# GLA recurrence then squared-ReLU FFN on one Trainium2 core: dense rows for q and k, on-chip transposes for the last decays of blocks 0 to 3, and another order of the opening

## The chip, the cores and the metric

The kernel runs on one core of a Trainium2 chip. The core has a matrix engine (TensorE, called PE in the profile, with its weight loads shown apart as PEld), three engines for elementwise work (VectorE or DVE, ScalarE or ACT, GpSimd or POOL), and SyncE (SP), which here only issues DMAs. The metric is the device time of one execution in microseconds (us); lower is better. Each engine works off its own instructions in the order in which the program lists them and waits on semaphores for the others, so the order of the program text is the order of work on every engine.

## What is computed

```python
def _attn_ref(q, k, v, alpha):                 # each [4, 8, 768, 48], float32
    B, H, S, D = q.shape
    state = np.zeros((B, H, D, D), dtype=np.float32)
    for t in range(S):
        state = alpha[:, :, t, :, None] * state + np.einsum('bhd,bhe->bhde', k[:, :, t], v[:, :, t])
        y[:, :, t] = np.einsum('bhd,bhde->bhe', q[:, :, t], state)

def _moe_ref(x, w_in, w_out):                  # x = y as [3072, 384]; 384 -> 2048 -> 384
    h = np.maximum(x @ w_in, 0.0)
    return (h * h @ w_out).astype(np.float32)
```

The two weights arrive as float64; the queries, keys, values and alphas as float32.

## The kernel before

**Blocks.** The 768 steps of a sequence are cut into 6 chunks of 128 steps (C). A block n is one chunk of one of the 4 batches, so there are 24 blocks, and blocks 0 to 3 (GB = 4) are the first chunk of all batches. A block works with its 128 steps on the partitions and its 8 heads of 48 columns in the free dimension. Four blocks make a group of 512 tokens; the FFN runs group by group, and the attention of the next group is woven into the FFN of the current one.

**The steps of a block.** With b the running product of the alphas inside the chunk, these are, by the names that the hand-written list uses:
- `load`: DMAs from SP of alpha (a), q, k and v of the block, 192 KB each (L109).
- `ln` (L244): ACT takes the logarithm of alpha. `cs` (L265): TensorE sums the logarithms over time by one matmul with a triangular matrix of ones, into a PSUM bank of 512 columns, of which the sums fill 384. `eb` and `ei` (L276, L280): ACT takes exp of plus and minus the sums, which are b and 1/b (`inv`).
- `mq` and `mk` (L284): DVE multiplies q by b and k by 1/b in place.
- `bl` and `br` (L297, L303): the last row of b is the decay of the state over the whole chunk. It is needed with the 48 key dimensions on the partitions, a column for each head pair. `bl` writes the row (1536 bytes) from SBUF to a row in DRAM, and `br` reads it back with two DMAs into `last`, transposed by its addresses. All three are issued by SP.
- `kT`, `qT` (L309): four TensorE transposes each, of 128x128, so that two heads of 64 columns (48 used) make one transpose; `kc`, `qc` (L325) copy the result from PSUM to SBUF, on DVE for block 0 and on ACT otherwise.
- `sc` (L372) multiplies keys by queries, `am` (L380) is DVE's masked copy of these scores, `kv` (L395) sums keys by values, `us` (L406) adds the state before the chunk on DVE, and `st` (L420, L421) forms the new state on DVE: it adds the second half of the sums and multiplies by `last`.
- `ya`, `yb` (L352): y of two blocks on TensorE, in two parts with a hop through POOL (L456) between them. `ev` (L515) copies this y from PSUM into x, the FFN's input, by six copies on DVE and the others on ACT for the pairs beginning with blocks 0 and 2.

**Dense and wide rows.** The transposes take 128 columns, two heads of 64, so q and k are kept in tiles of 8 heads of 64 columns, whose columns 48 to 63 POOL sets to zero once at the start (L97 and its like). The loads of q and k write 48 of every 64 columns of such a tile; the loads of a and v write tiles of 384 columns without gaps. Blocks 2 and 3 borrow their tiles from pools that the FFN uses later.

**The FFN.** Its input weights come as 8 pieces of 128x768 in float64 (768 KB, `weights`). A piece is turned into float32 by three steps: `first` (L153, L157, two DVE operations on the high words), `middle` (L166, L169, two ACT operations) and `second` (L175, L179, L182, three DVE operations). The first layer of group 0 multiplies in float32 (`ffn_in`, L806): output row block j of 16 needs weight piece j/2 and the x of the whole group, three matmuls of 512 columns. For j = 0 and 1 each is split into a half for blocks 0 and 1 (`ha`) and a half for blocks 2 and 3 (`hb`), so that the first halves can run before the second y is there. Later groups use three-pass matmuls on parts of the operands (L623, L702), with the weights' parts kept in DRAM and streamed back. Relu and square of h are then done by ACT and DVE in one of several mixes (L638, L640, L652, L657, L661), named by the letters in `AT['tp']`, one letter for j modulo 4.

**The order.** The opening, up to the first full matmuls of the FFN, is the list `first` (lines 852 to 861): words such as `cs1` or `load3q`, called from left to right. For instance its last lines in the kernel before are

```python
        weights2 qT3 sc2 load4q qc3 kv2 second0 am2 br3 first1 sc3 weights3 us2
        load4a kv3 am3 us3 load4k middle1 ha1 second1 ya2 yb2 ev2 weights4 first2
        ha0 hb1 middle2 hb0 st2 st3 st1
```

`warm` and `zeros` (L221, L338) are matmuls on tiles of zeros whose result is never used; they fill TensorE's waits. After the list, `weave` walks through the FFN's units, each with a cost, and slips in the other work (attention of the next blocks, weight conversions) when the running cost passes a position. These positions are the numbers of the table `AT` in line 19.

## Time and profile before

The median of 3 runs is 519.17 us (518.97 to 519.44). The profile is of one execution of its own.

| quantity | us |
| --- | --- |
| time of the profiled execution | 519.41 |
| its span, first to last instruction | 517.6 |
| DMA q1, share of 16 engines over the span | 70.0% |

| stretch (us) | PE busy | DVE busy | ACT busy | POOL busy |
| --- | --- | --- | --- | --- |
| 0 to 5.6 | 4.33 | 1.83 | 1.80 | 4.74 |
| 5.6 to 14 | 6.44 | 4.36 | 4.47 | 0.60 |
| 14 to 36 | 19.58 | 18.62 | 12.37 | 0 |
| 140 to 254 | 113.66 | 93.28 | 77.89 | 0 |
| 254 to 514 | 259.98 | 161.93 | 131.24 | 0 |

Times inside an execution are counted from the start of the span. A line of a timeline gives the start, the duration of the run of instructions, the engine, the line of the kernel, the operation and its tiles, and in brackets how long the engine was idle just before and who ended that wait. A matmul's end is modelled, so a busy PE is not PE at its peak. The row PEclk of the page, the granted TensorE clock in tenths, is 9 (90% or more) throughout; the mean granted clock is 1.000. Loads are listed by tile with the time at which they landed; "lands" below is that time.

### The profile page before, as it was taken

Reading aid. Unit: us, or ns where it says so; the run is one execution under the profiler, and the core shown is the slowest. Engines: PE = TensorE matmul, PEld = TensorE weight load, DVE = VectorE, ACT = ScalarE, POOL = GpSimd, SP = SyncE. Lnnn points to the kernel's source line nnn. Section 1 sums busy time; section 2 is a strip of 40 time slices with the busy share of each in tenths; the row PEclk is TensorE's granted clock in tenths of the full one; section 3 lists DMA queues with packets and bytes.
Section 4 is the critical chain, followed back from the end, with each engine's and each line's share of the span. In section 5 each row is a group of like instructions: output and inputs, shape, how many; then the busy total and the mean of one; then the engine's idle time right before and its main releaser. Section 6 shows DMA issues by size and latency. Waiting matters only on the chain.

```text
span 517.6 us, 12956 instructions
## 1 busy us (share of the span) xinstructions
PE 508.0 (98%) x5292; PEld 420.5 (81%) x5292; DVE 370.0 (71%) x639; ACT 303.9 (59%) x638; POOL 5.3 (1%) x29
## 2 busy tenths in 40 slices
PE   7989999999999999999999999999999999999997
PEld 4754455668878689988899988899988899988996
DVE  4698989996898898875888176778165578164861
ACT  4658786766788766176954175955075754154620
POOL 4000000000000000000000000000000000000000
PEclk9999999999999999999999999999999999999999
DMA  9999777262699688898965888865774544898201
GB/s 158 206 267 219 209 232 227 61 185 110 220 262 208 186 214 217 294 334 200 272 158 176 253 241 210 231 161 152 247 241 124 183 126 151 271 349 290 66 1 62
DMA packets 141283, 103.15 MB, mean 199 GB/s; under 512 B 111508, under 2 KB 114600, under 8 KB 141224
## 3 DMA queue, kind: packets, MB, share of 16 engines
q1 hardware_dynamic: 141224, 102.32, 70.0%
q8 instruction: 42, 0.69, 0.6%
q14 instruction: 17, 0.14, 0.1%
HBM read 84.97 MB, written 17.33 MB: 198 GB/s over the span
## 4 chain that ended last, share of the span: by engine, by line
PE 91%; DMA 4%; ACT 2%; SPq 1%; DVE 1%; issue 0%; DVEq 0%
PE o L702 41%; PE h L623 31%; PE h L806 7%; PE y L352 4%; PE sckv L372 2%; PE T L482 2%; PE sckv L395 2%; DMA row<-b 1%; DMA a_lent<-in_alpha_dram 1%; DMA a_in<-in_alpha_dram 1%; DMA k_in<-in_k_dram 1%; PE cs L265 1%; DVE x L515 1%; PE cs L268 0%; PE cs L269 0%; SPq L109 0%
## 5 line engine op out<-in xcount | busy, mean ns | idle before, releaser
L638 ACT ACTIVATE hid<-h 128x512 f32<-128x512 f32 x40 | 24.0, 602 | 81.6 <-PE h L623 81.5
L623 PE MATMUL h<-xa,wb 128*128 128x512 f32 x240 | 68.3, 393 | 0.0
L623 PE MATMUL h<-xl,wl 128*128 128x512 f32 x240 | 67.6, 390 | 0.0
L623 PE MATMUL h<-xd,wd 128*128 128x512 f32 x240 | 67.2, 395 | 0.0
L515 ACT COPY x<-y 32x256 f32<-32x256 f32 (+2 forms) x132 | 47.5, 365 | 26.8 <-PE y L352 21.6
L702 PE MATMUL o<-wb,ha 128*128 128x384 f32 x168 | 57.4, 342 | 0.0
L702 PE MATMUL o<-wd,hd 128*128 128x384 f32 x320 | 56.4, 334 | 0.0
L702 PE MATMUL o<-wl,hl 128*128 128x384 f32 x168 | 56.2, 335 | 0.0
L702 PEld LDWEIGHTS o<-wd,hd 128*128 128x128 f32 x320 | 55.6, 188 | 0.0
L623 PEld LDWEIGHTS h<-xl,wl 128*128 128x128 f32 x240 | 45.0, 188 | 9.8
L623 PEld LDWEIGHTS h<-xd,wd 128*128 128x128 f32 x240 | 44.3, 188 | 9.5
L623 PEld LDWEIGHTS h<-xa,wb 128*128 128x128 f32 x240 | 44.6, 188 | 8.7
L702 PE MATMUL o<-wb,hx 128*128 128x384 f32 x152 | 51.3, 338 | 0.0
L702 PE MATMUL o<-wl,hx 128*128 128x384 f32 x152 | 50.8, 334 | 0.0
L806 PE MATMUL h<-x,w_in 128*128 128x512 f32 (+1 forms) x108 | 43.6, 552 | 1.2 <-ACT x L515 1.2
L702 PE MATMUL o<-w_out,hid 128*128 128x384 f32 x128 | 43.4, 491 | 0.0
L547 DVE TENSOR_TENSOR osb<-o,osb 128x384 f32<-128x384 f32 x24 | 13.2, 555 | 39.9 <-PE o L702 31.0
L547 DVE TENSOR_TENSOR hid<-h,hid 128x512 f32<-128x512 f32 x40 | 27.4, 687 | 18.9 <-PE h L623 18.8
L806 PEld LDWEIGHTS h<-x,w_in 128*128 128x128 f32 x108 | 19.9, 190 | 21.1 <-issue 17.2
L702 PEld LDWEIGHTS o<-w_out,hid 128*128 128x128 f32 x128 | 23.8, 190 | 15.3
L597 ACT ACTIVATE ha<-hid 128x512 fp32r<-128x512 f32 x42 | 26.6, 641 | 15.6 <-DVE hx L598 8.8
L598 DVE SCALAR_TENSOR_TENSOR hl<-ha,hid 128x512 fp32r<-128x512 f32 x42 | 28.7, 684 | 6.4 <-ACT ha L597 6.4
(113 smaller groups left out, 886.7 us busy)
## 6 DMA issues: line engine op xcount, KB each, us to landing
wd<-do SPq DMA_DIRECT2D x38, 384.0 KB, 4.3
wl<-lo SPq DMA_DIRECT2D x34, 384.0 KB, 3.9
wl<-li SPq DMA_DIRECT2D x32, 384.0 KB, 4.9
wd<-di SPq DMA_DIRECT2D x32, 384.0 KB, 5.0
raw<-in_moe_w_in_dram SPq DMA_DIRECT2D x8, 768.0 KB, 6.3
raw<-in_moe_w_out_dram SPq DMA_DIRECT2D x8, 768.0 KB, 6.8
v_in<-in_v_dram SPq DMA_DIRECT2D x24, 192.0 KB, 5.4
out_dram<-osb SPq DMA_DIRECT2D x24, 192.0 KB, 4.4
```

The lines of the kernel that those rows point to most:

```text
L352: ins = nc.tensor.matmul(out=ys[e][64 * half : 64 * half + D + G * e, m % 2, p // 2, t], lhsT=lhsT, rhs=rhs, start=(half, e) not in seen, ...
L372: nc.tensor.matmul(out=ps[e][HALF[h], 0, p, :], lhsT=ks[rows, p, HALF[h]], rhs=qs[rows, p, HALF[h]], start=True, stop=True, skip_group_che ...
L395: nc.tensor.matmul(out=ps[h][64 * e : 64 * (e + 1), 1, p, G:64], lhsT=tile_of("k", n)[HALF[h], 2 * p + e, :], rhs=tiles["v"][n % NV][HALF[ ...
L482: nc.tensor.transpose(out=ps[h][:, i, p, :], in_=rows[HALF[h], 128 * p : 128 * (p + 1)], identity=ident[HALF[h], HALF[h]],)
L515: copy(out=x[kk][to : to + m, t : t + 2], in_=blk[n]["y"][e][r : r + m, :, p // 2],)
L547: nc.vector.tensor_tensor(out=o, in0=x, in1=z, op=op)
L597: nc.scalar.activation(out=a, in_=x, func=AF.Copy, scale=NEAR * E)
L598: nc.vector.scalar_tensor_tensor(out=l, in0=a.bitcast(FP32), scalar=-1.0 / E, in1=x, op0=ALU.mult, op1=ALU.add)
L623: nc.tensor.matmul(out=acc["h", j], lhsT=here[w, "i", p][:, kk, jj * 128 : (jj + 1) * 128], rhs=x_parts[x][:, kk], start=start and kk == 0 ...
L638: nc.scalar.activation(out=hid[j], in_=x, func=AF.Copy, scale=E)
L702: nc.tensor.matmul(out=acc[t][:, 0:DM], lhsT=lhs[:, t * C : (t + 1) * C], rhs=rhs, start=start, stop=stop, skip_group_check=True,)
L806: nc.tensor.matmul(out=ps, lhsT=w[:, kk, c0 : c0 + 128], rhs=xT[g][kk][:, cols], start=(kk == 0), stop=(kk == KM - 1),)
```

## The change

For blocks 0 to 3 alone, q and k are loaded into new tiles `qk_dense` of 384 columns without gaps. `mq` and `mk`, which multiplied in place, now read the dense tile and write the tile of 64-column heads that the transposes read. b of these blocks goes to new tiles of 64-column heads, `b_wide`, with POOL setting the gaps of their last 32 rows to zero (four more memsets).

In place of `bl` and `br`, two new steps carry the last decays of these blocks. `lt` transposes the last 32 rows of b, four TensorE transposes from 32x128 to 128x32, into the 128 columns of the block's `cs` bank that the sums leave free. `lc` is one DVE copy of column 31 of each (128x4) into `last`. Four row DMAs and eight last DMAs are no longer issued. Later blocks keep `bl` and `br`.

The list `first` is written anew. Behind a, q and k of blocks 0 and 1, its loads go a2, v0, a3, v1, q2, k2, weights, k3, q3, v2, v3 (before: v0, a2, k2, v1, q2, a3, k3, weights, v2, q3, weights, v3), so that alpha of block 3 moves from the twelfth to the ninth load. `second1` moves behind `ev2`, `ha1` and `ha0` stand behind `yb2`, the four calls of `zeros2` (three filler matmuls each) become two, and the weights and the loads of block 4 are spread otherwise.

In `AT`, the positions of the conversions and splits move (for instance w_first from 43.79, 38.55, 78.67 to 44.75, 40.07, 81.86, w_in_at from 2.79 to 2.35, g0 from -0.77, 19.74, 25.33 to -0.77, 20.69, 27.02), the buffer limits room1 and room go from 24 and 25 to 25 and 24, ahead from 5 to 6, s0 from 2 to 3, and tp from DMAD to DDAD: of the groups from 2 on, four of 16 row blocks of h now take a copy by ACT, an addition by DVE (L547) and one DVE operation for Relu and square (L652), instead of a copy and a Relu by ACT and a square by DVE.

```diff
--- before.py
+++ after.py
@@ -16,7 +16,7 @@
 
 
 GB = 4
...
 
 
 RUN = {0: 128, 32: 32, 64: 64, 96: 32}
@@ -99,13 +99,22 @@
     def tile_of(x, n):
         return lent.get((x, n), tiles[x][n % len(tiles[x])])
 
+    dense = {
+        (x, n): flat(two_k("qk_dense", shape=(H, 64)))[:, 0 : H * D].rearrange("a (h d) -> a h d", h=H)
+        for x in "qk" for n in range(GB)
+    }
+
+
+    b_wide = [two_k("b_wide", shape=(H, 64)) for _ in range(GB)]
+    for t in b_wide:
+        nc.gpsimd.memset(t[C - 32 :, :, D:64], 0.0)
 
     srcs = {"a": alpha, "q": q, "k": k, "v": v}
 
     def load(n, xs="aqkv"):
         c, b = divmod(n, B)
         for x in xs:
-            t = tile_of(x, n)
+            t = dense.get((x, n), tile_of(x, n))
             nc.sync.dma_start(
                 out=t[:, :, 0:D] if x in "qk" else t.rearrange("a (h d) -> a h d", h=H),
                 in_=srcs[x][b, :, c * C : (c + 1) * C, :].rearrange("h s d -> s h d"),
@@ -272,8 +281,15 @@
         return blk[n]["cs"].rearrange("a p t -> a (p t)")[:, 0 : H * D]
 
     def eb(n):
-        b = blk[n]["b"] = p2.tile([128, H * D], FP32, tag="b", name="b")
+        if n < GB:
+            b = blk[n]["b_wide"] = b_wide[n]
+            b = blk[n]["b"] = b[:, :, 0:D]
+            sums = sums_of_logs(n).rearrange("a (h d) -> a h d", h=H)
+            nc.scalar.activation(out=b, in_=sums, func=AF.Exp)
+            return
+        b = p2.tile([128, H * D], FP32, tag="b", name="b")
         nc.scalar.activation(out=b, in_=sums_of_logs(n), func=AF.Exp)
+        b = blk[n]["b"] = b.rearrange("a (h d) -> a h d", h=H)
 
     def ei(n):
         inv = blk[n]["inv"] = p2.tile([128, H * D], FP32, tag="inv", name="inv")
@@ -282,25 +298,41 @@
     def scaled(x, n, factor):
         t = tile_of(x, n)[:, :, 0:D]
         nc.vector.tensor_tensor(
-            out=t, in0=t, in1=factor.rearrange("a (h d) -> a h d", h=H), op=ALU.mult
+            out=t, in0=dense.get((x, n), t), in1=factor, op=ALU.mult
         )
 
     def mq(n):
         scaled("q", n, blk[n]["b"])
 
     def mk(n):
-        scaled("k", n, blk[n].pop("inv"))
+        scaled("k", n, blk[n].pop("inv").rearrange("a (h d) -> a h d", h=H))
 
     def bl(n):
 
         if n // B < NCH - 1:
-            nc.sync.dma_start(out=rows_t[n], in_=blk[n]["b"][C - 1 : C, :])
+            nc.sync.dma_start(out=rows_t[n], in_=blk[n]["b"][C - 1 : C].rearrange("a h d -> a (h d)"))
 
     def br(n):
         if n // B < NCH - 1:
             row = rows_t[n].rearrange("a (p e d) -> (a d) e p", e=2, d=D)
             for e in range(2):
                 nc.sync.dma_start(out=last_t[n % 4][64 * e : 64 * e + D, :], in_=row[:, e])
+
+    def lasts(n):
+        ps = blk[n]["cs"].rearrange("a p t -> a (p t)")[:, H * D :]
+        return ps.rearrange("a (p t) -> a p t", p=NP)
+
+    def lt(n):
+        rows = slice(C - 32, C)
+        b = blk[n]["b_wide"].rearrange("a h d -> a (h d)")
+        for p in range(NP):
+            nc.tensor.transpose(
+                out=lasts(n)[:, p, :], in_=b[rows, 128 * p : 128 * (p + 1)],
+                identity=ident[rows, rows],
+            )
+
+    def lc(n):
+        nc.vector.tensor_copy(out=last_t[n % 4], in_=lasts(n)[:, :, 31])
 
     def turned(x, n):
         rows = tile_of(x, n).rearrange("a h d -> a (h d)")
@@ -837,7 +869,7 @@
             store(g, t, o)
 
 
-    steps = {f.__name__: f for f in (ln, sp, cs, eb, ei, mq, mk, bl, br, qT, qc, kT, kc, ev)}
+    steps = {f.__name__: f for f in (ln, sp, cs, eb, ei, mq, mk, bl, br, lt, lc, qT, qc, kT, kc, ev)}
     steps["sc"], steps["kv"], steps["am"] = scores, state_sums, masked
     steps["us"], steps["st"] = sums_copied, next_state
     steps["ya"], steps["yb"] = lambda n: ga(n, None), lambda n: gb(n, None)
@@ -850,14 +882,14 @@
     steps["hb"] = lambda j: ffn_in(0, j, slice(HT, 2 * HT))
     steps["first"], steps["middle"], steps["second"] = convert_first, convert_middle, convert_second
     first = """
-        ln0 cs0 ei0 mk0 warm0 eb0 bl0 mq0 kT0 load0v kc0 ln1 qT0 load2a load2k cs1
-        eb1 qc0 mq1 sc0 bl1 kv0 qT1 load1v ei1 mk1 load2q load3a kT1 ln2 qc1 load3k
-        cs2 br0 am0 kc1 eb2 sc1 weights0 br1 us0 kv1 zeros2 bl2 load2v am1 ei2 us1
-        load3q ya0 ln3 cs3 yb0 eb3 weights1 mk2 ei3 load3v mq2 qT2 st0 ev0 kT2
-        zeros2 zeros2 zeros2 kc2 first0 mk3 middle0 kT3 mq3 br2 load4v qc2 kc3 bl3
-        weights2 qT3 sc2 load4q qc3 kv2 second0 am2 br3 first1 sc3 weights3 us2
-        load4a kv3 am3 us3 load4k middle1 ha1 second1 ya2 yb2 ev2 weights4 first2
-        ha0 hb1 middle2 hb0 st2 st3 st1
+        ln0 cs0 ei0 load2a warm0 eb0 mk0 mq0 kT0 qT0 load0v ln1 load3a cs1 load1v
+        load2q eb1 lt0 kc0 lc0 qc0 sc0 ei1 ln2 mq1 mk1 load2k weights0 qT1 kT1 lt1
+        am0 load3k kc1 qc1 kv0 us0 sc1 load3q kv1 am1 cs2 ln3 eb2 us1 ei2 cs3 ya0
+        lc1 load2v mq2 yb0 st0 load3v mk2 ei3 qT2 eb3 zeros2 ev0 first0 mk3 mq3 kT2
+        zeros2 kT3 kc2 qT3 middle0 weights1 qc2 load4v kc3 lt3 second0 sc2 qc3
+        weights2 load4q kv2 sc3 am2 kv3 am3 us2 us3 lt2 first1 lc3 weights3 weights4
+        middle1 lc2 ya2 yb2 load4a ev2 load4k ha1 ha0 second1 first2 middle2 st1 st2
+        st3 hb1 hb0
     """
     for word in first.split():
         f = max((x for x in steps if word.startswith(x)), key=len)
```

More of the change, by code (lines that the diff above doesn't have):

```diff
@@ L18 @@
 GB = 4
-AT = {'evs': 0.4, 'lead': 4, 'post': 3, 'w_first': (43.79, 38.55, 78.67), 'wstep': 2.35, 'w_in_at': 2.79, 'w_in_by': 2.29, 'room1': 24, 'room': 25, 's0': 2, 'ahead': 5, 'late': 2, 'xs': 0.26, 'g0': (-0.77, 19.74, 25.33), 'sc0': (2.36, 2.26, 2.42), 'g1': (7.27, 14.88, 26.94), 'g': (2.3, 18.45), 'g1x': 50.61, 'gx': 39.83, 'g0x': 56.03, 'k0': 2, 'h0': 15, 'k1': 6, 'h1': 1, 'h1by': 2, 'evs0': 0.66, 'tp': 'DMAD', 'tp1': 'ADDA', 'split': 8, 'o0': (40.23, 45.84), 'o1': (), 'o2': (20.83, 17.87, 30.43, 30.7, 43.15, 44.92), 'str1': 11.0, 'ga': 8.59, 'gb': 12.23}
+AT = {'evs': 0.4, 'lead': 4, 'post': 3, 'w_first': (44.75, 40.07, 81.86), 'wstep': 2.27, 'w_in_at': 2.35, 'w_in_by': 2.58, 'room1': 25, 'room': 24, 's0': 3, 'ahead': 6, 'late': 10, 'xs': 0.37, 'g0': (-0.77, 20.69, 27.02), 'sc0': (2.36, 2.26, 2.42), 'g1': (7.27, 14.88, 26.94), 'g': (2.3, 18.42), 'g1x': 49.43, 'gx': 39.86, 'g0x': 56.03, 'k0': 2, 'h0': 15, 'k1': 6, 'h1': 0, 'h1by': 2, 'evs0': 0.6, 'tp': 'DDAD', 'tp1': 'ADDA', 'split': 8, 'o0': (42.32, 49.42), 'o1': (), 'o2': (20.98, 18.02, 30.58, 28.47, 43.3, 45.07), 'str1': 12.04, 'ga': 8.64, 'gb': 12.15}
 RUN = {0: 128, 32: 32, 64: 64, 96: 32}
```

## The prediction

> **What bounds the kernel now.** I read the page's busy table first, then the chain of waits, then the timeline of the opening by engine, and last the table by stretches.
>
> ```profile
> span 517.6 us, 12956 instructions
> PE 508.0 (98%) x5292; PEld 420.5 (81%) x5292; DVE 370.0 (71%) x639; ACT 303.9 (59%) x638; POOL 5.3 (1%) x29
> ```
>
> TensorE is busy for 98%, so only its idle time, or work listed on it, can change the end. The timeline of PE shows where its last long wait of the opening ends:
>
> ```profile
> 33.81 0.70 PE L806 MATMUL h<-x,w_in 128*128 128x256 f32 x2 [0.71 <-ACT x L515]
> 34.79 0.70 PE L806 MATMUL h<-x,w_in 128*128 128x256 f32 x2 [0.29 <-ACT x L515]
> 35.68 7.14 PE L806 MATMUL h<-x,w_in 128*128 128x256 f32 x20 [0.19 <-ACT x L515]
> ```
>
> From 35.68 us on it runs almost without a gap (the stretch 36 to 140 us has 104.00 us of PE in 104.00, with 89.46 of DVE); the one later wait is 0.34 us, at 148.28. So the kernel is an opening of 35.68 us, 478.3 us of dense TensorE work, and 3.6 us of tail. The diff leaves the dense matmuls alone; it can act on the opening, and on whether the dense part stays dense. The marker I follow is the first cumulative sum of block 4 (L265), at 42.66 us, which closes the 7.14 us stretch above.
>
> What orders the opening: the chain of waits has
>
> ```profile
> 11.30 5.52 DMA a_lent<-in_alpha_dram
> 16.84 0.53 ACT a_lent L244
> 17.42 0.91 PE cs L265 x2
> 18.33 0.66 PE y L352 x31
> ```
>
> The alpha of block 3 arrives at 16.82, and TensorE, which works in listed order, does its sums before the second half of y. After y DVE sets the pace, and late in the opening it does weights first:
>
> ```profile
> 19.01 2.66 DVE L515 COPY x<-y 32x256 f32<-32x256 f32 x6 [0.67 <-PE y L352]
> ...
> 29.46 0.34 DVE L406 TENSOR_TENSOR us<-sckv,s 128x192 f32<-128x192 f32 x1
> 29.72 0.94 DVE L175 SCALAR_TENSOR_TENSOR power<-raw,power 128x768 uint32<-128x768 uint32 x1
> 30.59 0.95 DVE L179 SCALAR_TENSOR_TENSOR w_in<-upper,w_in 128x768 f32<-128x768 uint32 x1
> 31.57 0.96 DVE L182 TENSOR_TENSOR w_in<-w_in,power 128x768 f32<-128x768 f32 x1
> 32.56 2.67 DVE L515 COPY x<-y 32x256 f32<-32x256 f32 x6
> ```
>
> The second y is done near 31.6 (its last matmul starts at 31.38), but its copies start at 32.56 with no wait named: DVE was still converting a weight.
>
> **The change, part by part.** Times "after" below are my estimates from these rows.
>
> *Transfers.* The SP queue loses four row and eight last issues. In before, the first pair of last holds SP from 13.41 for 2.71 us. Loads of 192 KB land 1.09 us apart early on (v of block 0 at 10.64, alpha of block 2 at 11.73, k of block 2 at 12.82). The first data move at 1.82 and a load lands 1.3 us after its turn. Alpha of block 3 becomes the ninth load: 1.82 + 9 x 1.09 + 1.3 = 12.9. v of block 1 stays tenth: 14.0 (before 13.8). The first raw takes 3.3 us (its packets run from 17.28 to 20.61). So k of block 3 lands near 20.6, q 21.7, v of block 3 at 23.9, where before TensorE waited for that v until 27.19. Whether dense rows move faster is not shown: all of these loads have packets of 192 B. The nearest rows are the landings early on, 0.98 us apart for dense targets (a, v) and 1.13 for wide ones (q, k). Four of these come before v of block 1: 0 to 0.6 us. I take 0, since the packets are the same.
>
> *POOL.* Four memsets more stand ahead of the identity and the causal mask, 0.14 us each (the L97 row: three in 0.49): the mask comes at 4.5 instead of 3.94 and the first sums start 0.5 us later than at 4.20. Nothing of it is left at 13.8, where v of block 1 is what TensorE waits for.
>
> *First y.* us of block 1 ends at 15.57, as now. TensorE does two sums first (0.84 each, from 14.5 to 16.1), y 1.16 (15.92 to 17.08 now), the POOL hop 0.13, and 0.69: 18.1 instead of 19.0.
>
> *DVE, in the new listing, from 18.1:* copies 2.66 (20.8), first0 0.94 (21.7), mk3 and mq3 0.47 each (22.6; both inputs have landed), second0 2.73 as now from 24.20 to 26.93 (25.4), am2 and am3 0.66 each (26.7), us2 and us3 0.38 each (27.5). Now us3 ends at 29.8 because first1 stood ahead of it and v was late. The second y ends 1.8 us after us3 (31.6 less 29.8): 29.3. Meanwhile DVE does first1 (0.94) and two lc. No row shows lc; it lies between 0.06 (the 128x1 memset) and 0.34 (L406, 128x192 out of PSUM), and I take 0.15, near L406 less its elements. Both ends fit before 29.3. The copies run from 29.3 to 32.0, second1 comes behind them.
>
> *TensorE from 29.3:* four half units of 1.3 us (six passes of 215 ns; now one is done at 27.8, one at 31.54). The third one's last input is ACT's copy, 0.4 behind DVE's: 32.4, when TensorE wants it at 32.8. They end at 34.5. The next unit needs weight 1: second1 takes 2.8 (29.72 to 32.53 now), so 32.0 + 2.8 = 34.8. Then 12 passes of 0.43: the marker comes at 40.0 instead of 42.66, **2.66 us earlier**.
>
> *lt and zeros.* The 16 small transposes are bounded by 8 x 32 L482 rows (32 in 1.15, so 0.15 for four) and the L309 ones (0.66 for four). Three of the four groups stand in idle time of TensorE, the third delays scores by at most 0.6, under the 0.9 that am2 waits for second0. Six filler matmuls (0.43 each) go; they filled waits. The waits this adds: lc of block 0 on DVE waits for its transposes, which stand behind the sums of block 1 on TensorE, and behind lc is the copy of block 0's q, for which its scores wait (9.19 now, about 10.4 then). The v of block 0 goes from seventh to eighth load, 1.82 + 8 x 1.09 + 1.3 = 11.8 (now 10.64), so its us slips from 12.15 to about 12.7. Behind both stands only what waits for v of block 1 at 14.0 anyway.
>
> *Later.* M turns to D at 16 places: DVE 0.68 more (L652), ACT less; from 214 to 254 us DVE is busy for 28.82 of 40, so it is covered. The rest of the list (weights, splits) is moved by one to three units. What is late next is DVE: when second1 is done, both orders have done ev2 and two weights, at 35.2 in before and 34.8 in after (four lc were added). TensorE is 2.66 ahead but DVE only 0.4. Weight 2: first2 0.94, six state steps 2.1, second2 2.7, so 40.5; TensorE wants it at 40.0 + 0.65. From there a weight takes DVE 3.7 and TensorE 5.15, so the lead grows again. At 148.28 there is no slack at all now (0.34 of wait on L284). I allow 0.4 lost.
>
> **Sum.** The profiled execution took 519.41, its span 517.63. 519.41 - 2.66 + 0.4 = 517.15; it lies 0.24 over the median of 519.17, so **517.0** in round numbers.
>
> **Clock.** TensorE starts slow: the L221 matmuls take 0.85 to 1.0 us each until about 5 us and L338's, of the same shape, 0.43 later, while PEclk reads 1.00. After that no gap in before exceeds 0.86; in after I find up to 1.3 (before the first y). [...]
>
> **Rivals.**
> 1. *DVE takes over.* TensorE gains 2.66, and the later stages run at DVE's lead of 0.4. For it: 89.46 of 104 us busy, no slack at 148.28. Against: 14.5 us of DVE idle there, and its weight work is listed later. Time: 519.17 - 0.4 = 518.8. Chance 0.17.
> 2. [...] Chance 0.10; another 0.03 for slower by other ways.
> 3. *Dense rows do speed up the loads,* and no stall comes: 517.0 - 0.4 - 0.6 = 516.0. Chance 0.06.
> 4. *The shift of transfers does nothing,* because loads take 1.2 us each: v of block 3 lands at 25.5, against 25.4 needed. It costs nothing, so it has no time of its own.
>
> **How the numbers follow.** The forecast has 0.64. A measurement here can tell about 0.2%, 1.04 us. Faster (under 518.1): 0.64 + 0.06 = 0.70. Same: rival one, 0.17. Slower: 0.13. The range goes from 515.8 (rival three and a shorter lc) to 519.2 (past rival one); it leaves out rival two.
>
> **What would show it.** Right: the copies of the second y start near 29.3 with no weight op between us3's and them but first1; the marker is at 40.0; PE idle after it stays under 1 us; no L303 in SP before 40 us. Wrong: matmuls of 0.8 us among the fillers after 14 us (clock), waits of PE on DVE between 40 and 150 us (rival one), or alpha of block 4 landing after 39.5, which would hold the marker itself.

## The result: slower by 0.9%, and with a spread that the kernel before does not have

Over 14 runs the changed kernel takes 525.03 us (median; 520.50 to 527.54), the kernel before 519.23 (518.97 to 520.13). The ratio is 1.0094, 95% interval 1.0069 to 1.012. The forecast was 517.0 with a range of 515.8 to 519.2, so the sign was wrong: it expected 2.2 us less and it became 5.8 us more.

### The profile after

The profiled execution took 525.82 us. From its page, the busy table and the row of the granted clock (TensorE's clock in tenths, in 40 slices of 13 us):

```profile
span 523.8 us, 12971 instructions
...
PE 511.4 (98%) x5296; PEld 424.3 (81%) x5296; DVE 379.6 (72%) x659; ACT 297.6 (57%) x622; POOL 6.1 (1%) x33
...
PEclk9789999999999999999999999999999999999999
```

TensorE is as full as before, 98%, but of a longer span, and it has 3.4 us more of busy time for the same dense matmuls, 16 small transposes more and six fillers fewer. The second and third digit of the clock row point to the reason: there the clock was not full. The table by stretches of the same kernel (length, busy time of PE, PEld, DVE, ACT and POOL with counts, then the granted clock, the DMA share and GB/s) puts borders on it:

```profile
14.00:19.90 5.90, 3.95 (x146) 2.82 (x139) 3.10 (x9) 2.61 (x7) 0.00 (x0) 1.00 1.19 255
19.90:26.73 6.83, 6.00 (x60) 5.05 (x60) 3.96 (x10) 2.20 (x6) 0.00 (x0) 0.50 0.91 253
26.73:36.96 10.23, 7.40 (x249) 6.44 (x247) 6.35 (x15) 5.40 (x8) 0.00 (x0) 1.00 0.80 224
36.96:40.38 3.42, 3.42 (x8) 2.71 (x9) 3.20 (x7) 2.47 (x7) 0.00 (x0) 0.50 0.00 0
```

Two stretches, of 6.83 and 3.42 us, ran at a clock of 0.50. In the kernel before the clock is 1.00 from 5.8 us to the end of the work. What stands ahead of each is seen in TensorE's timeline (the bracket gives the idle time just before and who ended it; "issue" means that nothing which the profile shows was waited for):

```profile
17.16 0.69 PE L384 MATMUL y<-qs,us 48*48 48x64 f32 x32
17.65 0.50 PE L384 MATMUL y<-am,v_in 64*48 64x64 f32 x18
20.62 1.94 PE L384 MATMUL y<-am,v_in 64*64 64x64 f32 x46 [2.48 <-issue]
...
33.57 0.42 PE L384 MATMUL y<-am,v_in 64*48 64x64 f32 x11
35.58 1.37 PE L384 MATMUL y<-am,v_in 64*48 64x64 f32 x52 [1.59 <-issue]
36.88 12.28 PE L838 MATMUL h<-x,w_in 128*128 128x256 f32 x36
49.00 0.81 PE L274 MATMUL cs<-a_in,causal 128*128 128x384 f32 x2
```

In both y's, in the middle of a row of matmuls with the same kind of operands, TensorE stops for 2.48 and 1.59 us without waiting for any engine or load. The clock falls within the first gap (at 19.90 us; the gap ends at 20.62) and 1.4 us after the second (at 36.96). The first sums of block 4, the marker of the prediction, come at 49.00 us instead of 42.66, 6.34 later. Matched from the end, every later matmul of the dense part is 6.34 to 6.41 us late, apart from some between 80 and 171 us, where the order of the work has changed: the whole loss arises in the opening, and the new positions in `AT` and the new `tp` together cost 0.07 us.

DVE only passes this on. Its copies of the two y's (L547) wait for TensorE:

```profile
22.62 2.65 DVE L547 COPY x<-y 32x256 f32<-32x256 f32 x6 [3.78 <-PE y L384]
...
37.01 2.67 DVE L547 COPY x<-y 32x256 f32<-32x256 f32 x6 [2.74 <-PE y L384]
```

The new order did what it was said to do: no conversion of a weight stands right ahead of the second copies any more (before, they came at 32.56, directly behind one), and DVE stood idle for 2.74 us there. But the y itself was late.

### The profile page after: what moved, and what is told of

Read it like the earlier page. It is cut to its first block, busy times and chain, and to the rows that moved or that the text cites. A ratio compares the mean times of both kernels' runs of the same rounds, so it can differ in the third digit from the quotient of the medians.

```text
span 523.8 us, 12971 instructions
## 1 busy us (share of the span) xinstructions
PE 511.4 (98%) x5296; PEld 424.3 (81%) x5296; DVE 379.6 (72%) x659; ACT 297.6 (57%) x622; POOL 6.1 (1%) x33
## 4 chain that ended last, share of the span: by engine, by line
PE 94%; DVE 2%; ACT 1%; issue 1%; POOL 1%; POOLq 0%; DVEq 0%
PE o L734 40%; PE h L655 31%; PE h L838 8%; PE y L384 5%; PE sckv L404 2%; PE T L514 2%; PE sckv L427 2%; PE cs L274 1%; PE cs L278 1%; PE zeros L370 0%; PE cs L277 0%; PE qT L341 0%; PE kT L341 0%; DVE am L412 0%; ACT ks L357 0%
## 5 line engine op out<-in xcount | busy, mean ns | idle before, releaser
L670 ACT ACTIVATE hid<-h 128x512 f32<-128x512 f32 x56 | 33.5, 600 | 92.3 <-PE h L655 90.0
L579 DVE TENSOR_TENSOR hid<-h,hid 128x512 f32<-128x512 f32 x56 | 38.5, 689 | 33.6 <-PE h L655 33.5
L547 ACT COPY x<-y 32x256 f32<-32x256 f32 (+2 forms) x132 | 47.3, 366 | 23.5 <-PE y L384 14.0
L684 DVE SCALAR_TENSOR_TENSOR hid<-hid 128x512 f32<-128x512 f32 x56 | 37.3, 684 | 0.0
L838 PEld LDWEIGHTS h<-x,w_in 128*128 128x128 f32 x108 | 21.4, 201 | 19.3 <-issue 16.3
L734 PEld LDWEIGHTS o<-w_out,hid 128*128 128x128 f32 x128 | 23.9, 190 | 15.5
```

The lines of the kernel that those rows point to most:

```text
L547: copy(out=x[kk][to : to + m, t : t + 2], in_=blk[n]["y"][e][r : r + m, :, p // 2],)
L579: nc.vector.tensor_tensor(out=o, in0=x, in1=z, op=op)
L670: nc.scalar.activation(out=hid[j], in_=x, func=AF.Copy, scale=E)
L684: nc.vector.scalar_tensor_tensor(out=h, in0=h, scalar=0.0, in1=h, op0=ALU.max, op1=ALU.mult)
L734: nc.tensor.matmul(out=acc[t][:, 0:DM], lhsT=lhs[:, t * C : (t + 1) * C], rhs=rhs, start=start, stop=stop, skip_group_check=True,)
L838: nc.tensor.matmul(out=ps, lhsT=w[:, kk, c0 : c0 + 128], rhs=xT[g][kk][:, cols], start=(kk == 0), stop=(kk == KM - 1),)
```

## The theories

The page's list of DMA queues has a queue that no line of the kernel issues:

```profile
q8 instruction: 42, 0.69, 0.6%
```

That is 42 packets of 16 KB in an execution; TensorE has 10,752 records in the trace (weight loads, matmuls, semaphore instructions), 256 for each packet (best1, one of the kernels below, has 256 records more and 43 packets). Counted from 0 in the order of their start, the two gaps stand ahead of record **449** and record **961**, which is 512 apart.

**Theory A, pieces of instructions.** TensorE's instructions come in pieces of 256 records, one packet of q8 each. My assumption is that the piece that begins with record 449 + 256 k is asked for when the piece before it is begun (record 193 + 256 k) and waits behind transfers that were issued earlier: here record 193 runs at 14.07 us, the first packet starts at 17.93 and record 449 runs at 20.62. The new list packs the small matmuls closer (records 705 to 960 run in 3.33 us, 4.59 in the kernel before), so TensorE uses up a piece in less time than the next one takes; then it idles, and the clock falls after it.

**Rival B, fillers.** The clock falls because filler matmuls were taken out, and the gap is beside the point. **Rival C, this y.** The gap belongs to this y: its operands, or the hop through POOL. **Rival D, pace alone.** Pieces, but what the transfers do does not matter.

## The experiments

Every ratio is to the kernel before in the same batch (medians of 519.2 to 519.6). "Marker" is the first sums of block 4 in the profiled execution, as a difference to 42.66 us. Gaps are given only where they stand at a record 449 + 256 k (or the one behind it).

| kernel | median us (range) | ratio, 95% interval | marker | late pieces: record, gap in us |
| --- | --- | --- | --- | --- |
| changed kernel | 525.03 (520.50 to 527.54) | 1.0094, 1.0069 to 1.012 | +6.34 | 449: 2.48; 961: 1.59 |
| shift148 | 530.82 (527.50 to 532.80) | 1.021, 1.0169 to 1.0251 | +8.82 | 449: 2.93; 705: 0.35; 961: 0.73; 1217: 0.30; 5569: 1.80; 6337: 0.58 |
| shift60 | 533.17 (531.57 to 536.55) | 1.0275, 1.023 to 1.0321 | +1.71 | 961: 2.61; 3777: 2.40; 4545: 2.73; 7361: 1.45; 8129: 1.35; 9153: 0.81 |
| raw_late | 524.45 (523.17 to 525.02) | 1.0091, 1.0072 to 1.0109 | +3.58 | 449: 0.56; 961: 2.91 |
| zeros4 | 528.76 (526.98 to 529.59) | 1.0172, 1.0148 to 1.0197 | +6.33 | 449: 0.62; 961: 2.56; 3777: 1.81 |
| spread | 522.51 (521.06 to 524.56) | 1.0061, 1.004 to 1.0083 | +2.96 | 449: 0.62; 961: 2.25 |
| spread_shift | 527.02 (523.59 to 528.18) | 1.013, 1.0091 to 1.0169 | +4.32 | 5569: 1.74; 6337: 0.58 |
| parts | 524.90 (523.20 to 525.28) | 1.0094, 1.0076 to 1.0112 | +3.04 | 961: 1.23; 3777: 2.06 |
| order_only | 524.03 (523.67 to 524.82) | 1.0087, 1.0071 to 1.0104 | +4.37 | none over 0.3 |
| before_shift60 | 524.09 (523.24 to 525.59) | 1.009, 1.0071 to 1.0109 | -0.18 | 3777: 2.23; 4545: 0.35; 7361: 1.44; 8129: 0.34 |
| shift148b | 527.33 (526.79 to 527.88) | 1.0149, 1.0134 to 1.0164 | +3.43 | 705: 0.44; 961: 0.31; 1217: 3.24; 5569: 1.77; 6337: 0.36 |
| best1 | 525.82 (523.55 to 527.40) | 1.0115, 1.0081 to 1.0149 | +5.59 | 1217: 0.80 |
| gate | 520.43 (519.04 to 524.78) | 1.0034, 1.0009 to 1.0059 | +4.59 | 449: 0.83 |
| gate_order | 520.18 (518.42 to 520.80) | 1.0007, 0.9998 to 1.0017 | -0.72 | 961: 0.88 |
| gate_fill | 520.79 (518.92 to 522.04) | 1.0023, 1.0011 to 1.0035 | +0.04 | 449: 0.91; 3777: 1.18 |

After 12 us, not one gap of 0.3 us or more that the profile marks "issue" stands at another record in these kernels; every other one has an engine or a load as its releaser. The times that I gave for theory A ahead of the runs were less good: the median lies above my range in twelve of the fourteen kernels, and only order_only and before_shift60 lie within it. What the theory foretold better is at which records a gap can stand.

### Moving the records, not the program: shift148 and shift60

```diff
-    for _ in range(3):
+    for _ in range(2):
         warm(0)
+    ticks = ps_att.tile([128, NP, 64], FP32, tag="att", name="ticks")
+    for i in range(38):                     # shift148; 16 in shift60
+        rows = slice(64 * (i % 2), 64 * (i % 2) + 64)
+        nc.tensor.matmul(
+            out=ticks[rows, 0, 0:48], lhsT=s_t[0][rows, 0, :], rhs=s_t[0][rows, 1, 0:48],
+            start=True, stop=True, skip_group_check=True,
+        )
```

> Edit: the third start-up filler matmul is replaced by 38 tiny matmuls of zeros with zeros (result unused), so that TensorE's instruction stream is 148 records longer ahead of everything else; nothing else moves. Theory A (instruction pieces): TensorE's instructions arrive by DMA in pieces of 16 KB, 256 records of the trace; the changed kernel stalls ahead of records 449 and 961, 512 apart, because the piece asked for near record 193 (14.07 us) waits behind the first weight transfer (2048-byte packets, 13.5 to 16.7 us) and starts only at 17.93. With 148 more records the piece is asked for near 10.3 us, ahead of the weight transfer: no stall in the first y, granted clock 1.0 from 10 us on, second y copies near 31 instead of 37.0 us, time 517.2 to 519.5. Rival B (the fillers that were taken out are missing, the clock falls by itself): the half-rate stretch from 19.9 us stays, 523 to 527. Rival C (the wait belongs to this y, its operands or the POOL hop): the 2.5 us gap stays ahead of the same y matmul, now record 597, 523 to 527.

> Edit: as the shift by 148, but with 16 tiny matmuls of zeros, 60 records. Theory A (instruction pieces): the stall stays ahead of the 449th record, which is now an earlier place of the program (record 389 of the changed kernel, a matmul of q with us, first part of y); the piece is asked for near 13.7 us, at the start of the weight transfer, so it still waits: a gap of 1.5 to 3 us, the clock falls, 522 to 527. Rival C (the wait belongs to this y): the gap stays at the same y matmul of am and v, which is now record 509. Rival B (fillers): the half-rate stretch near 20 us with or without the gap, 523 to 527.

The gaps moved in the program and stayed at their records. In shift148 the 449th record is now a matmul of the state sums, and the gap is there:

```profile
16.69 0.39 PE L434 MATMUL sckv<-v_in,k_in 64*64 64x48 f32 x14
20.02 0.88 PE L434 MATMUL sckv<-v_in,k_in 64*64 64x48 f32 x18 [2.93 <-issue]
```

In shift60 record 449 came without a gap; records 961 and, far behind the opening, 3777 are where it stops:

```profile
26.79 0.45 PE L391 MATMUL y<-qs,us 48*48 48x64 f32 x14 [0.86 <-DVE us L445]
29.85 0.70 PE L391 MATMUL y<-qs,us 48*64 48x64 f32 x17 [2.61 <-issue]
...
169.74 0.37 PE L391 MATMUL y<-am,v_in 64*48 64x64 f32 x9
172.51 0.57 PE L391 MATMUL y<-am,v_in 64*64 64x64 f32 x22 [2.40 <-issue]
```

Rival C falls. My numbers for theory A were wrong for both: for shift60 I had a gap of 1.5 to 3 us at record 449 and 522 to 527 us (no gap there, 533.17), for shift148 517.2 to 519.5 (measured 530.82). In shift148 record 193 came at 11.85 us instead of near 10.3, and the first weight had been issued at 11.68; the piece started at 17.46, right behind that weight's last packet (17.35). In shift60 record 193 came at 11.38, ahead of the weight's issue (11.58), and the piece started at 13.23. A fifth of a microsecond ahead of a transfer or behind it made 3.8 us of difference for the piece.

### Taking the transfer away, putting the fillers back: raw_late and zeros4

```diff
 # raw_late
-        am0 ... mk1 load2k weights0 qT1 ...  st0 load3v mk2
+        am0 ... mk1 load2k qT1 ...           st0 load3v weights0 mk2
 # zeros4
-        sc1 load3q kv1 am1 ...        zeros2 kT3
+        sc1 load3q kv1 zeros2 am1 ... zeros2 zeros2 kT3
```

> Edit: the first weight load of the list is moved behind load3v (four loads of 192 KB later); nothing else moves. Theory A (instruction pieces): at 14 us only loads with 192-byte packets are under way, as in the kernel before, where the piece started 0.9 us after it was asked for; the first stall (2.48 us) shrinks to under 0.5 us and the clock stays at 1.0 there; the second stall, behind a later weight, may stay; the first conversion starts later by up to 2 us. Time 518 to 522. Rival B (fillers): the half-rate stretch from 19.9 stays, 523 to 527. Rival C (this y): the gap stays, 523 to 527.

> Edit: the two calls of filler matmuls that the change took out are put back (one ahead of am1, one beside the one ahead of kT3), six matmuls of 0.43 us. Theory A (instruction pieces): the stalls stay ahead of records 449 and 961 (12 to 24 records earlier in the program), the clock falls, 522 to 527. Rival B (fillers): TensorE's clock stays at 1.0 after 10 us, no gap over 1 us, 516.5 to 518.5.

In raw_late the first gap shrank from 2.48 to 0.56, and the half-rate stretch that came with it is gone; the second grew to 2.91 and kept its own (33.52 to 36.94 us); the time of 524.45 is above my range of 518 to 522:

```profile
18.68 1.26 PE L384 MATMUL y<-am,v_in 64*64 64x64 f32 x46 [0.56 <-issue]
...
33.02 1.80 PE L384 MATMUL y<-am,v_in 64*48 64x64 f32 x52 [2.91 <-issue]
```

With all four calls of fillers back (zeros4) the time was no better. The 449th record was late by 0.62, since the fillers gave the piece more time, but the 961st by 2.56, with half rate from 33.91 to 40.73:

```profile
30.91 0.68 PE L384 MATMUL y<-qs,us 48*48 48x64 f32 x31 [0.85 <-DVE us L438]
34.15 0.26 PE L384 MATMUL y<-qs,us 48*64 48x64 f32 x1 [2.56 <-issue]
```

Rival B falls: raw_late has no first half-rate stretch without those fillers, zeros4 has the second with them. So does rival D, by the first piece: with record 193 at 14.05 in raw_late and 14.07 in the changed kernel, the packet starts at 15.93 and at 17.93. The table shows the two pieces that mattered; its times are those of the records and of the packets of queue q8 in the trace.

| kernel | record 193 runs | packet starts | records 448, 449 run | record 705 runs | packet starts | records 960, 961 run |
| --- | --- | --- | --- | --- | --- | --- |
| before | 12.76 | 13.65 | 16.74, 16.74 | 25.68 | 26.81 | 30.27, 30.28 |
| changed | 14.07 | 17.93 | 17.93, 20.62 | 30.44 | 33.23 | 33.77, 35.58 |
| raw_late | 14.05 | 15.93 | 17.91, 18.68 | 26.56 | 30.43 | 29.89, 33.02 |
| spread | 13.72 | 15.89 | 17.58, 18.42 | 26.57 | 29.72 | 29.96, 32.42 |
| gate_fill | 13.55 | 15.90 | 17.41, 18.53 | 25.33 | 26.27 | 29.13, 29.14 |

Where a record of the opening waited for its piece, it ran 2.3 to 3.0 us after the packet's start. In all the kernels the wait from the asking to that start was between 0.2 and 5.6 us in the opening. In the changed kernel the first weight's 2048-byte packets run from 13.58 to 16.58 us, and a load of k issued behind them lands at 18.22; the piece asked for at 14.07 starts at 17.93. That pieces stand in line behind data is inferred from such starts; no row shows the line itself. The bursts of small matmuls use up 256 records in 3.3 to 3.9 us (30.44 to 33.77, 14.07 to 17.93), so, with the 2.3 to 3.0 us from a packet's start to its first record, a piece that was not under way within about a microsecond (3.3 less 2.3) was late, by this estimate.

### The kernel before, 60 records later: before_shift60

```diff
 # before.py; nothing else differs
-    for _ in range(3):
+    for _ in range(2):
         warm(0)
+    # and 16 matmuls of zeros, as in shift60
```

> Edit: the kernel before, untouched but for its third start-up filler matmul, which becomes 16 tiny matmuls of zeros (60 records more, result unused). Theory A (instruction pieces): every piece now begins 60 records earlier in the program, so in the later groups pieces begin inside y, as in the changed kernel with the same shift (gaps of 2.4, 2.7, 1.5 and 1.4 us near 170, 196, 321 and 351 us there, all at records 449 + 256 k); the clock falls behind some of them: 523 to 530, without any change of the work. If the pieces did not matter, the 60 records cost under 1 us: 518.5 to 520.

The plainest of the experiments: no work, no order and no transfer was changed, the opening was as fast (marker -0.18), and the kernel lost 4.6 us, more than three quarters of what the change lost. Its timeline in the third group, and that of the kernel before:

```profile
167.62 0.45 PE L363 MATMUL y<-am,v_in 64*48 64x64 f32 x14
170.30 0.47 PE L363 MATMUL y<-am,v_in 64*64 64x64 f32 x17 [2.23 <-issue]
```

```profile
167.84 0.68 PE L352 MATMUL y<-am,v_in 64*48 64x64 f32 x31
168.45 2.37 PE L623 MATMUL h<-xd,wd 128*128 128x512 f32 x9
```

The granted clock stayed at 1.00 in the profiled execution, so this is the cost of late pieces alone: the four gaps in the table add up to 4.36 us.

### Halves of the change: parts and order_only

```diff
 # parts: the list and AT of before, with lt and lc for bl and br
-        eb1 qc0 mq1 sc0 bl1 kv0 qT1 ...    cs2 br0 am0 kc1 ... br1 us0
+        eb1 lt0 qc0 lc0 mq1 sc0 kv0 qT1 ... kT1 lt1 ... cs2 am0 lc1 kc1 ... us0
 # order_only: the list and AT of after, with bl and br for lt and lc
-    dense = {(x, n): ... for x in "qk" for n in range(GB)}
+    dense = {}
```

> Edit: the dense rows and the last decays by TensorE (lt, lc in place of bl, br) alone, in the listing and with the positions of the kernel before. Theory A: the stalls come from the new listing, which packs the small matmuls and moves the first weight transfer ahead; here the packing is nearly that of before, so gaps at records 449 and 961 stay under 1 us: 517.5 to 520.5. If the new steps themselves cost (memsets, lt, lc on the path of the first y), 520 to 523 without any gap at those records.

> Edit: the new listing and positions alone, with the old wide rows and the old trip of the last row through DRAM (bl and br stand where lt and lc stand in the new list). Theory A: the small matmuls are packed as in the changed kernel (32 records fewer), so gaps of 1 to 3 us at records 449 and 961 stay and the clock falls: 521 to 528. If the new steps are what costs: 516.5 to 519.5.

Each half alone costs about as much as the whole. In parts I expected almost none of it; but the transposes change the count of records, and record 961 (1.23, with half rate behind it) and record 3777 (2.06) came late. In order_only the time was in the range that I gave, but not for my reason: no piece was late by over 0.3. With the four row and eight last DMAs back in SP's queue, k of blocks 2 and 3 landed late: k of block 2 was issued at 15.28 (10.59 in the changed kernel), behind the first last DMAs, and landed at 18.41. DVE stood idle for 1.35 us for the one and 0.31 for the other, with the copies of y in between, and TensorE waited for what came of it:

```profile
18.50 0.56 DVE L294 TENSOR_TENSOR k_in<-k_in,inv 128x384 f32<-128x384 f32 x1 [1.35 <-DMA k_in<-in_k_dram]
...
23.12 0.56 DVE L294 TENSOR_TENSOR qk_lent<-qk_lent,inv 128x384 f32<-128x384 f32 x1 [0.31 <-DMA qk_lent<-in_k_dram]
```

```profile
23.82 0.63 PE L335 MATMUL kT<-ident,qk_lent 128*128 128x128 f32 x4 [2.69 <-ACT ks L351]
```

Behind this gap, which has nothing to do with pieces, the clock was at half from 25.23 to 38.88 us. So here the clock fell behind a gap of another origin (2.69 us), without a late piece.

### Trying to get the pieces in time: spread, spread_shift, shift148b, best1

```diff
 # spread
-  load2k weights0 qT1 ... load3v mk2 ... qc3 weights2 load4q ... lc3 weights3 weights4 ... ev2 load4k
+  load2k qT1 ... load3v weights0 mk2 ... qc3 load4q ... lc3 weights2 ... ev2 load4k weights3 weights4
 # spread_shift: spread, and 40 ticks in place of the three warm; shift148b: the 40 ticks alone
 # best1: spread, the 40 ticks, 27 more behind hb0, one row of ks written to DRAM (gate2); and
-  ev0 first0 mk3 mq3 ... qT3 middle0 weights1 qc2 ... second0 sc2 qc3 ... us2 us3 lt2
+  ev0 mk3 mq3 first0 ... qT3 qc2 ... lt3 gate2 weights1 sc2 qc3 middle0 ... us2 us3 second0 lt2
```

> Edit: the weight loads of the opening are listed later: the first behind load3v, the third (weights2) behind lc3, the fourth and fifth behind the second y; all else as in the changed kernel. Theory A, sharpened by the first four runs (a piece of 256 records is asked for when the one before it is begun; it starts 0.9 to 1.0 us later if little stands in the queues, later if transfers issued before it are still under way, and its instructions run 2.4 to 3.0 us after its start): piece for record 449 as in raw_late, a gap of 0.5 to 0.8; piece for record 961, asked for near 26.5, starts within 1.5 us instead of 3.9, so the gap of 2.9 us shrinks to under 1.0, and the clock stays at 1.0 after 10 us. Time 517.5 to 520. Rival D (the gaps come from how fast TensorE uses up 256 records, whatever the transfers do): the gap at record 961 stays above 2 us, 522 to 525.

> Edit: as spread, and the three start-up fillers are replaced by 40 tiny matmuls of zeros (148 records more, result unused), so that the records 449 and 961 fall on the transposes and fillers between the two bursts of small matmuls. Theory A: the opening has no gap over 0.8 us at a piece's first record, the start is later by 1 to 2.5 us because the tiny matmuls run at the low clock, later stages may get gaps where a piece's first record now falls into a y. Time 518 to 523, the opening's share of the loss under 3 us. Rival D: gaps of over 1.5 us at records 449 or 961 stay.

> Edit: the changed kernel with its three start-up fillers replaced by 40 tiny matmuls of zeros (148 records more, as spread_shift, but with the weight loads where the changed kernel has them). Theory A: record 193 comes near 10.0 us, ahead of the first weight's issue at 11.6, so the piece for record 449 starts by 11.5 and no gap stands there, unlike the first shift by 148, which asked at 11.85; the piece for 705 waits behind the weight and starts near 17.5 to 19, gap under 1.5 us in the fillers; the one for 961 may wait: 0 to 2.5 us. Later gaps near 237 and 268 us as in spread_shift (about 2.3 us and a clock fall). Time 521 to 527; the first y's copies on DVE start by 19.5 instead of 22.6 us.

> Edit: the changed kernel with 148 records of tiny zero matmuls in place of the start-up fillers, 108 more behind hb0 (256 in all, so the later pieces begin where they do in the changed kernel), the weight loads later (the second held back by a one-row DMA that waits for kc of block 2), mk3 and mq3 ahead of first0, middle0 behind qc3, second0 behind us3. Theory A with the listing's promise: no gap over 1 us after 14 us and a clock of 1.0, second y's copies by 31 us, the first sums of block 4 by 42 to 43.5 us (42.66 before, 49.00 in the changed kernel), time 517 to 520. If gaps at records 705 or 961 stay, 521 to 525.

Spread took the marker from +6.34 to +2.96, but its piece for 961 still stood behind a weight (26.24 to 29.25 us) and the gap there was 2.25, not under 1.0. Gap and time (522.51) are what rival D had on record for it; what speaks against rival D at this piece is gate, below, where no weight stood ahead of it. With 148 records put ahead, spread_shift and shift148b have no gap over 0.5 at the first pieces, as theory A says; in shift148b record 449 came at 14.98 without a gap, its piece having been asked for at 10.06 and started at 11.01. But the shift moved later borders into the y's of later groups (5569, 6337), and in shift148b into the first layer:

```profile
30.52 0.92 PE L847 MATMUL h<-x,w_in 128*128 128x256 f32 x3
34.67 1.65 PE L847 MATMUL h<-x,w_in 128*128 128x256 f32 x3 [3.24 <-issue]
```

In spread_shift TensorE instead waited 2.02 us for a transpose's input, which stood on DVE behind a weight that came late, and the clock was at half until 38.26. Best1 missed its aim: its second y began at 26.98 us (29.29 before), but then came gaps of 1.01 (a weight from DVE), 0.80 (record 1217) and 1.53 (the second lot of ticks read a state that DVE had not written yet) and two half-rate stretches.

### Is the listing faster where the pieces come: gate, gate_order, gate_fill

```diff
 # gate: spread, and weights2 waits for us3
-  lt2 first1 lc3 weights2
+  lt2 first1 lc3 gate3 weights2            # gate: one row of us written to DRAM by SP
 # gate_order: gate, and
-  ev0 first0 mk3 mq3 ... qT3 middle0 weights1 ... second0 sc2 qc3 ... us3 lt2
+  ev0 mk3 mq3 first0 ... qT3 weights1 ... sc2 qc3 middle0 ... us3 second0 lt2
 # gate_fill: gate_order, and
-  lc2 ya2 yb2
+  lc2 zeros2 ya2 yb2
```

> Edit: as spread, and the third weight load of the opening (weights2) is held back by a one-row DMA that waits for us of block 3. Theory A: the piece for record 961, asked for near 26.5 us, now has no weight transfer ahead of it and starts by 28.0 instead of 29.7, its gap falls from 2.25 to under 0.7; no gap over 1.2 us is left after 14 us, so the clock stays at 1.0; the first sums of block 4 near 41.5 to 42.5 us (before 42.66, changed kernel 49.00), time 517.5 to 519.5. Rival (the listing itself is slower even without late pieces): no such gap, and the sums of block 4 after 43.5 us, over 520.

> Edit: as gate, and in the list mk3 and mq3 stand ahead of first0, middle0 behind qc3, second0 behind us3, so that DVE and ACT no longer wait for the first weight ahead of the second y's inputs. Theory A: second y starts near 26.5 to 27.5 us, but the piece for record 961 is then asked for earlier too (near 24.5) and may wait for the second weight's transfer (to 25 us): gap 0 to 1.5 us; first sums of block 4 at 40.5 to 43 us, time 516.5 to 520. The rival as for gate.

> Edit: as gate_order, and three filler matmuls (one call of zeros2, 12 records) stand ahead of the second y, where TensorE waited 0.86 us for us of block 3 and then 0.88 us for record 961. Theory A: the fillers (1.3 us) take the place of both gaps, the second y ends no later than 30.9 us, and the half-rate stretch of 3.4 us behind it is gone; first sums of block 4 at 39.8 to 40.8 us (41.95 in gate_order, 40.0 forecast for the change), time 516.8 to 518.2. Rival (the listing is not faster even at full clock, since runs of gate_order with a granted clock of 1.0 took 519.1 to 520.6): the first sums of block 4 by 41 us but 519 to 520.5 in time, with the loss in gaps after 140 us.

In gate the piece for 961 started 0.24 us after it was asked for (3.16 in spread) and no gap stood there. Its twelve runs fall into groups: six with a granted clock of 1.0 took 519.04 to 520.02, five with 0.987 to 0.989 took 523.13 to 524.78 (one with 0.997 took 520.85); the profiled one is of the latter five, with a gap of 2.58 at a transpose whose input stood behind the first weight. Gate_order removed that wait, and its profile has the marker ahead of the kernel before, at 41.95, though one gap of a late piece and one half-rate stretch (28.81 to 32.22) were left:

```profile
26.99 0.66 PE L384 MATMUL y<-qs,us 48*48 48x64 f32 x30 [0.86 <-DVE us L438]
...
28.78 2.15 PE L384 MATMUL y<-am,v_in 64*48 64x64 f32 x52 [0.88 <-issue]
30.85 11.26 PE L838 MATMUL h<-x,w_in 128*128 128x256 f32 x36
41.95 0.81 PE L274 MATMUL cs<-a_in,causal 128*128 128x384 f32 x2
```

Gate_fill put fillers where those two gaps were. Both gaps and the half-rate stretch went, as expected, and the second y ended 0.3 us earlier; the marker did not follow, because there the weights' conversion on DVE set the pace. DVE was 0.95 us behind gate_order from the first y on (its copies began at 19.85, in gate_order at 18.90), since record 449 came 0.91 us late here and only 0.10 in gate_order:

```profile
29.11 1.49 PE L384 MATMUL y<-am,v_in 64*48 64x64 f32 x62
30.82 6.42 PE L838 MATMUL h<-x,w_in 128*128 128x256 f32 x24 [0.23 <-DVE w_in L191]
37.45 5.42 PE L838 MATMUL h<-x,w_in 128*128 128x512 f32 x12 [0.20 <-DVE w_in L191]
42.70 0.81 PE L274 MATMUL cs<-a_in,causal 128*128 128x384 f32 x2
```

It then lost 1.18 us at record 3777, a border that the fillers' 12 records had moved to an earlier place of the program (0.17 in gate_order). Its time of 520.79 is above what theory A (516.8 to 518.2) and the rival (519 to 520.5) had. None of the versions beats the kernel before; gate_order equals it.

## Why the prediction was wrong

| step | forecast us | measured us |
| --- | --- | --- |
| alpha of block 3 lands | 12.9 | 11.98 |
| v of block 1 lands | 14.0 | 12.86 |
| v of block 3 lands | 23.9 | 21.51 |
| first y starts | 16.1 | 17.16 |
| copies of the first y | 18.1 | 22.62 |
| us of block 3 ends | 27.5 | 33.2 |
| copies of the second y | 29.3 | 37.01 |
| first sums of block 4 | 40.0 | 49.00 |
| change from there to the end | +0.4 | +0.07 |

**The step that failed** is "First y", where the sum ran "y 1.16 [...], the POOL hop 0.13, and 0.69: 18.1", and again where the second y was put 1.8 us behind us of block 3. Both took TensorE's work as ready to run once its operands are there. No term stood for the arrival of the instructions, although the page lists their queue and the bursts of small matmuls, 32 from 17.16 to 17.65 us, are where they ran out. From there the miss of 9.0 us at the marker is made up, in size, of the two gaps (2.48 + 1.59 = 4.07) and the two half-rate stretches, which double what is busy in them (six filler passes take 2.77 us in the first and 1.46 behind it): 6.00 / 2 = 3.00 and 3.42 / 2 = 1.71. That is 8.78; the first y also began 1.06 us late. The sum says that the sizes fit; not every microsecond of it lies on the path, since some of the matmuls in the first stretch are fillers.

**Rival two**, a fall of the clock, had a chance of 0.10 in the prediction. The event was right: the clock did fall, 3.0 + 1.7 us worth, and the sign that was named for it was there: three fillers (six passes) took 2.77 us from 23.40 on. The reason behind the chance, that idle time ahead of the first y (14.5 to 16.1 us in the forecast) would bring it on with fewer fillers, was my assumption, and no run shows it: in the changed kernel the clock fell in the first gap inside a y and behind the second (at 19.90 and 36.96 us), and in zeros4, with the fillers back, it was at half from 33.91 to 40.73.

**Transfers** were misjudged on the good side: with dense rows the ten loads from q of block 0 to q of block 2 landed 0.99 us apart (4.99 to 13.92) where the sum had 1.09, so every load came earlier than forecast. Rival three's mechanism was there: order_only, with the same order and wide rows, has v of block 1 landed at 13.38 where the changed kernel has 12.86, 0.5 us of the 0 to 0.6 that the prediction allowed and took as 0. It bought nothing, as v of block 1 was no longer what TensorE waited for.

**The added waits** were costed at nothing behind v of block 1. Scores of block 0 began at 11.72, not 10.4, and the first y at 17.16, not 16.1, although v of block 1 was there at 12.86; between them TensorE idled for 0.19 us only. The wait for lc and the copy of q (TensorE idle for 1.01 us ahead of the scores) was foreseen. What was not is the clock, which was full only from 9.66 us on (from 5.79 before). Gate has the same list up to there but for one weight load, and in its profiled execution the clock was full from 4.44 us on; with the same 1.01 us of idle time its scores began at 10.03 and its first y ahead of the forecast:

```profile
15.48 0.69 PE L384 MATMUL y<-qs,us 48*48 48x64 f32 x32
```

Spread, whose list is gate's up to there, has 8.96, so the list up to there does not decide when the clock becomes full. The added waits were sized about right; the 1.1 us are the clock's.

**Later stages** came out as forecast in that the lag of the marker reached the end and `AT` made no difference. Rival one was not put to the test: TensorE came late, not early, so DVE had time to spare.

**What stays open** is whether the new order would give its 2.66 us if pieces and clock allowed. Gate_order's profile, 0.72 ahead with one half-rate stretch (1.7 us) and a gap of 0.88 still in it, speaks for it; gate_fill, without both, was held by DVE, but only behind a late piece of 0.91 us in the first y, so it does not decide. Against it, runs of gate_order at full clock took 519.12 to 520.56. No run of any version reached 517.0; the lowest is 518.42 (gate_order).

## What to carry to other kernels

In the changed kernel 256 records of small matmuls went in 3.3 to 3.9 us, against 12.5 us on the average of the execution (523.8 / 42), and a record that waited for its piece ran 2.3 to 3.0 us after the packet's start. With a burst like this, look up where the pieces begin (here at records 449 + 256 k) and which large transfer is under way when the record 256 earlier runs. A few records more moved these borders for the rest of the kernel: 60 of them cost 4.6 us in before_shift60, and 12 took the gap at record 3777 from 0.17 (gate_order) to 1.18 us (gate_fill). So a change of order must be judged by these borders and not by operands alone. A gap of "issue" inside a row of like matmuls was the sign (2.48 and 1.59 us in the changed kernel), and a stretch of 0.50 in the granted clock, in the gap or behind it, was the second half of the bill (3.00 and 1.71 us).

## What the runs showed of the hardware

- TensorE's instructions came in packets of 16 KB, 42 in an execution (43 in best1), each for 256 records. A late piece cost up to 3.24 us (shift148b) and stood at record 449 + 256 k, or the one behind it, in every kernel that had one. In the opening none of the first four packets of any kernel starts before the piece ahead of it is begun (record 193 + 256 k runs): in the changed kernel record 193 runs at 14.07 us and its packet starts at 17.93, record 705 at 30.44 and 33.23. Later, among long matmuls, packets start up to 46 records ahead of that record (shift148), so there the asking ran ahead of the execution.
- For these first packets the time from record 193 + 256 k to the packet's start was 0.2 us at the least (gate) and 5.6 at the most (shift148), and the packet then took 0.9 to 2.1 us of its own.
- The clock fell to 0.50 for 3.41 us (gate_order, 28.81 to 32.22), 6.83 (changed kernel, 19.90 to 26.73) or 13.65 (order_only, 25.23 to 38.88) at a time. A half-rate stretch followed gaps of 0.86 and 0.88 us, 0.9 us apart, in gate_order, and none followed 2.23 us at 170 us in before_shift60 or 2.40 us at 173 us in shift60. So the length of one gap alone does not explain when the clock fell. What else counts stays open.
- The clock became full between 4.44 us (gate) and 10.02 us (zeros4) of the profiled executions, with 8.96 in spread, whose list is gate's up to there.
- The clock goes with the spread: of the changed kernel's 14 runs, those with a mean granted clock of 0.997 took 520.50 to 522.05 us, those with 0.993 took 523.54 to 525.41, those with 0.990 took 525.82 to 527.54. One half-rate stretch of 3.41 us takes 0.33% off the mean clock of 518 us (3.41 / 2 / 518).
